# Retention attention and two feed-forward layers on one core: all attention ahead, and a second product that follows its first by two slices

## The chip, the cores and the metric

The kernel runs on one core of one Trainium2 chip. The metric is device microseconds of one execution, the median of several runs. The engines are named as the profile names them: PE does matrix products (PEld is its weight loads), DVE and POOL do elementwise work, ACT does activations and copies, SP issues the transfers (DMA).

## What is computed

A retention attention (2 batches, 8 heads, 768 positions, head size 64) is followed by two feed-forward layers over the 1536 resulting tokens of 512 features, with 2048 hidden features each. Cut to what matters:

```python
state = gamma * state + outer(k[:, :, t], v[:, :, t])     # for each t, batch and head
y[:, :, t] = scale * (q[:, :, t] @ state)
x = y as (1536 tokens, 512)
h = x @ w_in;   g = h * sigmoid(h);         x = g @ w_out      # layer 0
h = x @ w_in;   g = maximum(0.01 * h, h);   out = g @ w_out    # layer 1
```

## The kernel before, in words

**Attention** goes in 12 chunks of 128 positions, six of batch 0 and then six of batch 1. For a chunk, `scores` makes k times q on PE (16 small products), `masked` multiplies them by the decay mask `M` on DVE into `P`, `values` makes P times v, then state times q (not in the first chunk of a batch), then the state's increment k times v (not in the last chunk). `prep` scales q by `G` and k by `KD` on POOL, and a third POOL instruction (line 216) decays the state. `state` and `store_x` are the endings on DVE and ACT: the new state, and the output split into a rounded part `xh` and a rest `xl`. The chunk's q, k and v come in two halves of 512 KB into a ring of four chunks (`att_t`).

**The feed-forward part** treats the tokens as three sets of 512 and the hidden features as 16 slices of 128. For a layer, set and slice, `up` is the first product (12 matmuls of 512 columns, since both operands are split into a rounded part and a rest and three of the four combinations are taken), `act` is the activation on ACT and the split of its result `g` (rest on DVE), `down` is the second product (12 matmuls, four groups of three). After slice 15, `finish` takes the four sums away.

**Weights** arrive as 64-bit numbers, one block of 512 KB for a slice and product. `load_w` fetches a block into one of three stages `ws`, `words` takes its two words on ACT, `conv` makes a 32-bit number of them in four DVE instructions (lines 140, 144, 148, 152), `split_w` splits it (copy on ACT, line 157, and rest on DVE, line 158). `keep_w` writes the split block to scratch in DRAM, and later sets of the same layer read it back with `fetch_w`. There are 64 blocks to convert.

**The order** is written out by hand: each engine runs what the program lists for it, one after the other. Four chunks of attention come first. Then steps `s` follow: step `s` has the first product number `s` (layer, set, slice counted through), and the second product number `s - 20` (`LAG` is 20). The remaining eight chunks are woven into steps 0 to 16, one for two steps. The first 16 steps thus use 16 new blocks, one for each `up`, and there is no second product before step 20. The slots for `g` (20) and for weights (9) are two rings of equal tiles; eight of these tiles are the attention's ring before.

Of the kernel before, what the change touches and what calls it, by code (L numbers as in the profile page):

```python
# [18 lines left out]
C = 128  # L19
# [10 lines left out]
NU = 2 * SETS * NF  # L30
NA = 2 * (NCHUNK - CS)
LAG = NF + 4
WARM = 16
# [9 lines left out]
def retention_moe_kernel(ctx: ExitStack, tc: tile.TileContext, att, w1, w2, cst, out):  # L43
# [21 lines left out]
    cs = const.tile([128, NCST], F32, name="cs")  # L65
# [5 lines left out]
    G = cs[:, o + H + NP:NCST]  # L71
    M = const.tile([128, 2, NP * C], F32, name="M")

    st = [const.tile([128, NP, D], F32, name=f"st{i}") for i in range(2)]
# [6 lines left out]
    gring = [gs.tile([128, 2, T], FR, name=f"g{i}") for i in range(NF)]  # L81
    wring = [gs.tile([128, 2, 512], FR, name=f"w{i}") for i in range(5)]

    def widen():
        a = [gs.tile([128, 2, 512], FR, tag=f"r{i}", name=f"gw{i}") for i in range(8)]
        gring.extend(a[:4])
        wring[0:0] = a[4:]

    def next_w():
        wring.append(wring.pop(0))  # L90
        return wring[-1]
# [9 lines left out]
    def att_t(n, i):  # L101

        return raw[n % 4 * 2 + i // 2][:, i % 2]

    def load_att(n, *halves):
        for i in halves:
            nc.sync.dma_start(out=raw[n % 4 * 2 + i], in_=att[n, :, 2 * i:2 * i + 2])
# [13 lines left out]
    def fetch_w(w):  # L121
        W[w] = next_w()
        nc.sync.dma_start(out=W[w].bitcast(F32), in_=scr[w])
# [30 lines left out]
    def split_w(w):  # L154
        r = rs.pop(w)[0].bitcast(F32)
        t = W[w] = next_w()
        nc.scalar.activation(out=t[:, 0], in_=r, func=AF.Copy)  # L157
        nc.vector.tensor_tensor(out=t[:, 1], in0=r, in1=t[:, 0].bitcast(F32), op=ALU.subtract)  # L158
# [3 lines left out]
    LATE = 3  # L162

    def prep(n):

        if n >= LATE:
            nc.gpsimd.tensor_tensor(out=att_t(n, 0), in0=att_t(n, 0), in1=G, op=ALU.mult)
        if n % NC != NC - 1:
            k3 = att_t(n, 3).rearrange("p (h d) -> p h d", h=H)
# [4 lines left out]
    def scores(n):  # L174
        q, kT = att_t(n, 0), att_t(n, 1)
        sc = pt[n] = pair(n % 2)
# [6 lines left out]
    def masked(n):  # L183
        P = pp.tile([128, 2, NP * C], F32, tag="P", name="P")
        nc.vector.tensor_tensor(out=P, in0=pt[n], in1=M, op=ALU.mult)  # L185
        pt[n] = P

    def values(n, i):
        q, v = att_t(n, 0), att_t(n, 2)
        first = n % NC == 0  # L190
        P = pt.pop(n)
        yu[n] = y, u = bank(i), bank(i + 1)
        for p in range(NP):
            c = slice(p * C, p * C + C)
            for r in range(2):
# [3 lines left out]
                    start=(p == 0), stop=(first and p == NP - 1),  # L199
                )  # L200
        if not first:
            for p in range(NP):
                c = slice(p * C, p * C + C)
                for r in range(2):
                    s = slice(64 * r, 64 * r + 64)
                    nc.tensor.matmul(  # L206
                        out=y[s, c], lhsT=st[0][s, p, :], rhs=q[s, c],
                        start=False, stop=(p == NP - 1),
                    )
        if n % NC == NC - 1:  # L210
            return

        kn = att_t(n, 3)
        u = u[:, 0:NP * D].rearrange("p (a d) -> p a d", a=NP)
        if not first:
            nc.gpsimd.tensor_tensor(
                out=st[1], in0=st[0], in1=GC.unsqueeze(2).to_broadcast([128, NP, D]), op=ALU.mult
            )
        for p in range(NP):
            for r in range(2):  # L220
                c = slice((2 * p + r) * D, (2 * p + r) * D + D)
                nc.tensor.matmul(
                    out=u[64 * r:64 * r + 64, p, :], lhsT=kn[:, c], rhs=v[:, c], start=True, stop=True
                )

    def state(n):
        if n % NC == NC - 1:
            return
        u = yu[n][1][:, 0:NP * D].rearrange("p (a d) -> p a d", a=NP)
        if n % NC:  # L230
            nc.vector.tensor_tensor(out=st[0], in0=st[1], in1=u, op=ALU.add)
        else:
            nc.vector.tensor_copy(out=st[0], in_=u)

    def store_x(n):
        b, c = divmod(n, CS)
        y = yu.pop(n)[0].rearrange("p (a i) -> p a i", a=NP)
        h, l = (x[b][:, :, c * C:c * C + C] for x in (xh, xl))
        if n < LATE:
# [10 lines left out]
    hs, ys = {}, []  # L250

    def place(u):

        return u // (SETS * NF), u // NF % SETS, u % NF

    def up(u):
        layer, b, f = place(u)
        w = W.pop((layer, 0, f))
        h = hs[u] = bank(2 + u % 2)
# [9 lines left out]
    def act(u):  # L269
        g = gring[u % LAG]  # L270
        h = hs.pop(u)
        gf = gp.tile([128, T], F32, tag="gf", name="gf")
        for t in (gf, g[:, 0, :]):
            if place(u)[0] == 0:
# [7 lines left out]
    def down(u, m):  # L282

        layer, b, f = place(u)
        w, g = W[layer, 1, f], gring[u % LAG]
        if u == 0:
# [10 lines left out]
    def finish(u, m):  # L297
        layer, b, f = place(u)
# [7 lines left out]
        r0 = b * T + m * 128  # L306
# [3 lines left out]
        nc.sync.dma_start(out=out[r0:r0 + 128, :], in_=o)  # L310
# [3 lines left out]
    uses = {}  # L314
    for u in range(NU):
        layer, b, f = place(u)
        uses.setdefault(u, []).append((b == 0, (layer, 0, f)))
        uses.setdefault(u + LAG, []).append((b == 0, (layer, 1, f)))
    NS = NU + LAG

    def split_at(s):
        return [w for new, w in uses.get(s, []) if new]

    def weights(s):

        for w in split_at(s + 4):
            load_w(w)
        for w in split_at(s + 1):
            keep_w(w)
# [144 lines left out]
```

## Time and profile before

| what | before |
|---|---|
| median of 3 runs | 598.32 us (598.28 to 598.65) |
| the profiled execution | 598.46 us |
| its span in the trace | 596.3 us |
| PE busy | 576.2 us, 97% of the span |
| DVE busy | 296.8 us, 50% |
| ACT busy | 230.2 us, 39% |
| POOL busy | 31.0 us, 5% |

The profiled execution is 0.14 us above the median, and 2.16 us of it lie outside the span. Shares are averages over stages that differ: DVE's 50% is made of a stretch in which it hardly rests and a long one in which it mostly waits. PE's busy time counts a matmul up to its modelled end, and ends overlap the next ones, so the time of one matmul is read from where the next begins.

### The profile page before, as it was taken

What the parts mean: (1) busy time and instruction counts of PE and PEld (TensorE: products, weight loads), DVE (VectorE), ACT (ScalarE), POOL (GpSimd) and SP (SyncE); (2) the same over time, 40 slices, a digit from 0 to 9 for tenths busy, and PEclk for the clock granted to TensorE, in tenths of its full rate; (3) what the DMA queues carried; (4) which work ended last, traced back from release to release, by engine and by line L of the source; (5) the groups of instructions that cost most, each with busy time, mean ns of one, the idle gap of its engine ahead of it and who ended that gap; (6) DMA issues with size and microseconds to landing.
All of it is one profiled execution on the core that took longest, in us unless ns stands there. A gap on an engine that the chain in (4) does not pass through costs nothing.

```text
span 596.3 us, 8059 instructions
## 1 busy us (share of the span) xinstructions
PE 576.2 (97%) x3024; PEld 474.0 (79%) x3024; DVE 296.8 (50%) x486; ACT 230.2 (39%) x422; POOL 31.0 (5%) x31
## 2 busy tenths in 40 slices
PE   8669898999999999999999999999999999999997
PEld 6558777888888888888888888888888788888885
DVE  3789999496666320136586632586665211011001
ACT  1247564465545321144555422654553222111001
POOL 2450242000000000000000000000000000000000
PEclk9889999999999999999999999999999999999999
DMA  8879983889886765657699777398876685551921
GB/s 322 336 248 321 338 294 143 317 309 359 287 284 219 250 246 198 222 201 274 220 328 325 245 266 282 132 363 309 290 282 213 234 293 189 199 177 59 392 79 71
DMA packets 42231, 150.82 MB, mean 253 GB/s; under 512 B 4688, under 2 KB 4688, under 8 KB 42192
## 3 DMA queue, kind: packets, MB, share of 16 engines
q1 hardware_dynamic: 42048, 149.97, 71.1%
q8 instruction: 24, 0.39, 0.3%
q10 hardware_dynamic: 144, 0.34, 0.2%
q14 instruction: 15, 0.12, 0.1%
HBM read 113.58 MB, written 36.70 MB: 252 GB/s over the span
## 4 chain that ended last, share of the span: by engine, by line
PE 83%; DVE 9%; DMA 5%; issue 1%; ACT 1%; POOL 0%; DVEq 0%; SPq 0%; ACTq 0%
PE b L263 37%; PE p L292 22%; PE b L292 22%; DVE w L158 2%; DMA att_t<-att_dram 2%; DVE r L148 2%; DVE P L185 1%; DMA scr<-w 1%; DVE r L144 1%; DVE r L152 1%; PE b L197 1%; DMA cs<-cst_dram 1%; PE b L206 1%; DMA out_dram<-ob 1%; DVE xl L246 1%
## 5 line engine op out<-in xcount | busy, mean ns | idle before, releaser
L263 PE MATMUL b<-xh,w 128*128 128x512 f32 x488 | 161.1, 394 | 5.0 <-ACT w L157 2.7
L278 DVE TENSOR_TENSOR g<-gf,g 128x512 fp32r<-128x512 f32 x80 | 55.5, 693 | 136.8 <-ACT g L277 91.6
L263 PEld LDWEIGHTS b<-xh,w 128*128 128x128 f32 x488 | 92.1, 189 | 26.0 <-ACT w L157 3.1
L263 PE MATMUL b<-xl,w 128*128 128x512 f32 x244 | 95.7, 392 | 0.0
L263 PE MATMUL b<-xh,gw 128*128 128x512 f32 x280 | 91.9, 389 | 0.0
L277 ACT ACTIVATE gf<-b 128x512 f32<-128x512 f32 x48 | 28.7, 598 | 133.4 <-PE b L263 133.4
L275 ACT ACTIVATE gf<-b 128x512 f32<-128x512 f32 x48 | 28.5, 594 | 94.7 <-PE b L263 92.5
L263 PEld LDWEIGHTS b<-xh,gw 128*128 128x128 f32 x280 | 52.5, 188 | 10.9
L263 PE MATMUL b<-xl,gw 128*128 128x512 f32 x140 | 54.5, 389 | 0.0
L263 PEld LDWEIGHTS b<-xl,w 128*128 128x128 f32 x244 | 46.2, 189 | 9.4
L148 DVE SCALAR_TENSOR_TENSOR r<-ws,r 128x512 int32<-128x512 int32 x64 | 45.8, 715 | 2.2
L152 DVE CUSTOM_DVE_ANT_0 r<-r,u 128x1024 uint16<-128x1024 uint16 x64 | 45.3, 707 | 2.7
L133 ACT ACTIVATE r<-ws 128x512 f32<-128x512 f32 x64 | 43.1, 673 | 4.5 <-DVE w L158 4.2
L158 DVE TENSOR_TENSOR w<-r,w 128x512 fp32r<-128x512 f32 x43 | 34.1, 793 | 20.4 <-ACT w L157 19.2
L134 ACT ACTIVATE u<-ws 128x512 int32<-128x512 uint32 x64 | 42.9, 670 | 0.0
L157 ACT ACTIVATE w<-r 128x512 fp32r<-128x512 f32 x43 | 27.2, 633 | 31.5 <-DVE r L152 31.5
L292 PE MATMUL p<-w,g 128*128 128x512 f32 x144 | 36.9, 390 | 0.0
L292 PE MATMUL b<-w,g 128*128 128x512 f32 x144 | 36.7, 389 | 0.0
L292 PE MATMUL b<-g,w 128*128 128x512 f32 x138 | 35.0, 389 | 0.0
L292 PE MATMUL p<-g,w 128*128 128x512 f32 x138 | 35.0, 389 | 0.0
L292 PEld LDWEIGHTS p<-w,g 128*128 128x128 f32 x144 | 26.9, 188 | 5.9 <-DVE ob L309 0.3
L292 PEld LDWEIGHTS b<-w,g 128*128 128x128 f32 x144 | 27.0, 188 | 5.7
(69 smaller groups left out, 680.6 us busy)
## 6 DMA issues: line engine op xcount, KB each, us to landing
w<-scr SPq DMA_DIRECT2D x71, 512.0 KB, 4.4
ws<-w_dram SPq DMA_DIRECT2D x64, 512.0 KB, 5.1
gw<-scr SPq DMA_DIRECT2D x57, 512.0 KB, 4.3
scr<-w SPq DMA_DIRECT2D x43, 512.0 KB, 3.3
att_t<-att_dram SPq DMA_DIRECT2D x24, 512.0 KB, 7.4
scr<-gw SPq DMA_DIRECT2D x21, 512.0 KB, 3.0
out_dram<-ob SPq DMA_DIRECT2D x12, 256.0 KB, 2.1
cs<-cst_dram ACTq DMA_DIRECT2D x1, 330.0 KB, 5.0
```

What stands on the lines that cost most here:

```text
L133: nc.scalar.activation(out=r.bitcast(F32), in_=t[:, :, 1].bitcast(F32), func=AF.Abs)
L134: nc.scalar.activation(out=u, in_=t[:, :, 0].bitcast(U32), func=AF.Copy, scale=2.0 ** -29)
L144: nc.vector.tensor_scalar(out=r, in0=r, scalar1=3, scalar2=0x3FFFFFF8, op0=ALU.logical_shift_left, op1=ALU.bitwise_and,)
L148: nc.vector.scalar_tensor_tensor(out=r, in0=t[:, :, 1], scalar=-0x40000000, in1=r, op0=ALU.bitwise_and, op1=ALU.bitwise_or)
L152: nc.vector.tensor_tensor(out=r, in0=r, in1=u, op=ALU.add)
L157: nc.scalar.activation(out=t[:, 0], in_=r, func=AF.Copy)
L158: nc.vector.tensor_tensor(out=t[:, 1], in0=r, in1=t[:, 0].bitcast(F32), op=ALU.subtract)
L263: nc.tensor.matmul(out=h, lhsT=w[:, tw, k * 128:k * 128 + 128], rhs=(xh, xl)[tx][b][:, k, :], start=(n == 0), stop=(n == 3 * NP - 1),)
L275: nc.scalar.activation(out=t, in_=h, func=AF.Silu)
L277: nc.scalar.activation(out=t, in_=h, func=AF.Prelu, alpha=0.01)
L278: return lambda: nc.vector.tensor_tensor(out=g[:, 1, :], in0=gf, in1=g[:, 0, :].bitcast(F32), op=ALU.subtract)
L292: nc.tensor.matmul(out=ys[m], lhsT=l, rhs=r, start=(f == 0 and n == 0), stop=(f == NF - 1 and n == 2),)
```

## The change

Attention comes first as a whole, with the batches in turn: chunk 0 of batch 0, chunk 0 of batch 1, chunk 1 of batch 0, and so on (`ORDER`). The sets of the feed-forward part are made of chunks in this new order, and `finish` writes each to its rows. Each batch has its own state. The state's decay becomes a step of its own (`decay`) ahead of `values`. `masked` of the next chunk comes ahead of the conversion and of the chunk's endings. Three weight blocks are converted within attention (in chunks 3, 5 and 7), and three more are loaded there. `G` is no longer part of the constants' transfer on ACT's queue but a transfer of 256 KB on SP's, after the first three halves.

The feed-forward part is a list of 192 products. In the first 16 slices of layer 0, `up` runs for set 0 and for set 1 with the same weight block, one after the other, and `down` of set 0 follows two slices behind; after that one `down` and one `up` alternate, and 18 `down` stand at the end. The blocks read back are 112 where they were 128. Conversion runs five products ahead of use, and so does the reading back. Slots for `g` and for weights come from one list of 29 free tiles, taken in the order in which they became free. Core of the diff:

```diff
-NU = 2 * SETS * NF
-NA = 2 * (NCHUNK - CS)
-LAG = NF + 4
-WARM = 16
+ORDER = [b * NC + c for c in range(NC) for b in range(B)]
+WARM = 20
+LATE = 3
+LAG = 2
+SPLIT = 5
+FETCH = 5
...
-    gring = [gs.tile([128, 2, T], FR, name=f"g{i}") for i in range(NF)]
-    wring = [gs.tile([128, 2, 512], FR, name=f"w{i}") for i in range(5)]
+    free = [gs.tile([128, 2, 512], FR, name=f"s{i}") for i in range(21)]
...
+    ups = [[(l, 0, b, f) for f in range(NF)] for l in range(2) for b in range(SETS)]
+    downs = [(l, 1, b, f) for l in range(2) for b in range(SETS) for f in range(NF)]
+    ahead = [list(t) for t in zip(ups[0], ups[1])]
+    ahead += [[t] for u in ups[2:] for t in u]
+    ops = []
+    for i in range(len(downs) + LAG):
+        ops += downs[i - LAG:i - LAG + 1] if i >= LAG else []
+        ops += ahead[i] if i < len(ahead) else []
...
+        nc.sync.dma_start(out=G, in_=cst[:, ncs:])
...
+        for j in range(NJ):
+            w = early[(j - 3) // 2] if j in (3, 5, 7) else None
+            if j + 1 < NJ:
+                prep(j + 1)
+                scores(j + 1)
+            decay(j)
+            values(j)
+            if j + 4 < NJ:
+                load_att(j + 4, 0, 1)
+            if j in (4, 6, 8):
+                keep_w(early[(j - 4) // 2])
+                load_w(early[(j - 4) // 2 + 3])
+            if w:
+                words(w)
+            if j + 1 < NJ:
+                masked(j + 1)
+            if w:
+                conv(w)
+            store_x(j)
+            state(j)
+            if w:
+                split_w(w)
```

**PE, from the fourth chunk on.** The names: `p` scores, `b` a result bank, `st` the state, `P` the masked scores, `xh` and `xl` the two parts of a set, `w` or `s` a weight tile. Before, the fourth chunk and then the first product:

```order
L181 MATMUL p_321<-att_t 128x128 x8
L197 MATMUL b_330<-P,att_t 64x128 x8
L206 MATMUL b_330<-att_t,st_83 64x128 x8
L222 MATMUL b_331<-att_t 64x64 x8
L263 MATMUL b_384<-xh_85,w_115 128x512
L263 MATMUL b_384<-xl_88,w_115 128x512
```

Now, on PE, the last two chunks and the first product:

```order
L190 MATMUL p_659<-att_t 128x128 x8
L206 MATMUL b_668<-P,att_t 64x128 x8
L215 MATMUL b_668<-att_t,st_84 64x128 x8
L206 MATMUL b_690<-P,att_t 64x128 x8
L215 MATMUL b_690<-att_t,st_86 64x128 x8
L263 MATMUL b_722<-xh_88,s_102 128x512
L263 MATMUL b_722<-xl_91,s_102 128x512
```

Twelve chunks stand ahead of the first product where four stood.

**DVE, around the first conversion of a weight block.** `r` is the number being made, `ws` its stage, `u` its low word. Before, the conversion stands ahead of the state and of the next chunk's mask:

```order
L246 TENSOR_TENSOR xl_88<-yg,xh_85 128x4x128
L140 TENSOR_SCALAR r<-r 128x512
L144 TENSOR_SCALAR r<-r 128x512
L148 SCALAR_TENSOR_TENSOR r<-ws,r 128x512
L152 ISA r<-r,u 128x1024
L231 TENSOR_TENSOR st_83<-st_84,b_225 128x256
L185 TENSOR_TENSOR P<-p_215,M 128x1024
```

Now, on DVE from the mask ahead of the first conversion on:

```order
L194 TENSOR_TENSOR P<-p_308,M 128x1024
L137 TENSOR_SCALAR r<-r 128x512
L141 TENSOR_SCALAR r<-r 128x512
L145 SCALAR_TENSOR_TENSOR r<-ws,r 128x512
L149 ISA r<-r,u 128x1024
L250 TENSOR_TENSOR xl_91<-b_318,xh_88 128x4x128
L237 TENSOR_TENSOR st_86<-st_87,b_319 128x256
L155 TENSOR_TENSOR s_102<-r,s_102 128x512
```

The mask moved ahead of the conversion; the state and the split stand behind it.

**DVE, once the first products run.** `g` and `gf` belong to `act`. Before, in steps with a chunk of attention, from one mask to the next:

```order
L185 TENSOR_TENSOR P<-p_466,M 128x1024
L140 TENSOR_SCALAR r<-r 128x512
L144 TENSOR_SCALAR r<-r 128x512
L148 SCALAR_TENSOR_TENSOR r<-ws,r 128x512
L152 ISA r<-r,u 128x1024
L278 TENSOR_TENSOR g_101<-gf,g_101 128x512
L158 TENSOR_TENSOR w_115<-r,w_115 128x512
L140 TENSOR_SCALAR r<-r 128x512
L144 TENSOR_SCALAR r<-r 128x512
L148 SCALAR_TENSOR_TENSOR r<-ws,r 128x512
L152 ISA r<-r,u 128x1024
L246 TENSOR_TENSOR xl_89<-b_530,xh_86 128x4x128
```

Now, on DVE in the first slices, the instructions of one slice (two `up`, one `down`):

```order
L137 TENSOR_SCALAR r<-r 128x512
L141 TENSOR_SCALAR r<-r 128x512
L145 SCALAR_TENSOR_TENSOR r<-ws,r 128x512
L149 ISA r<-r,u 128x1024
L155 TENSOR_TENSOR s_112<-r,s_112 128x512
L137 TENSOR_SCALAR r<-r 128x512
L141 TENSOR_SCALAR r<-r 128x512
L145 SCALAR_TENSOR_TENSOR r<-ws,r 128x512
L149 ISA r<-r,u 128x1024
L278 TENSOR_TENSOR s_113<-gf,s_113 128x512
L155 TENSOR_TENSOR s_114<-r,s_114 128x512
L278 TENSOR_TENSOR s_115<-gf,s_115 128x512
```

Two conversions and two rests of `g` remain, and the attention's instructions are gone from between them; three products of PE stand beside them where there were two and a chunk.

## Rows read from the trace of the kernel before

**Rows 1.** The page, its first part: busy time, share, instructions of each engine.
```profile
PE 576.2 (97%) x3024; PEld 474.0 (79%) x3024; DVE 296.8 (50%) x486; ACT 230.2 (39%) x422; POOL 31.0 (5%) x31
```

**Rows 2.** Stretches (us from the start): busy of each engine, granted clock, DMA share, GB/s.
```profile
5.00:9.60 4.60, 3.95 (x34) 3.61 (x34) 2.88 (x9) 0.00 (x0) 0.66 (x1) 1.00 1.00 361
9.60:17.70 8.10, 6.82 (x114) 5.91 (x112) 5.45 (x7) 1.79 (x3) 5.46 (x6) 1.00 1.02 403
...
20.70:24.40 3.70, 3.70 (x38) 3.20 (x40) 2.31 (x3) 1.15 (x2) 1.85 (x2) 0.57 1.03 412
...
42.00:112.61 70.61, 66.55 (x617) 53.81 (x616) 64.19 (x100) 41.41 (x75) 13.59 (x11) 1.00 0.79 277
60.00:70.00 10.00, 8.56 (x74) 6.82 (x72) 9.70 (x15) 5.82 (x12) 3.75 (x3) 1.00 0.97 342
112.61:592.40 479.79, 479.54 (x2114) 396.16 (x2112) 204.86 (x345) 177.33 (x328) 0.00 (x0) 1.00 0.70 246
592.40:596.30 3.90, 0.00 (x0) 0.00 (x0) 0.42 (x1) 0.38 (x1) 0.00 (x0) 1.00 0.28 104
```

**Rows 3.** PE in order of time, the opening: start, us, instruction, count [idle before <-releaser].
```profile
5.65 3.98 PE L181 MATMUL p<-att_t 64*128 64x128 f32 x32 [1.00 <-DMA att_t<-att_dram]
9.56 1.41 PE L197 MATMUL b<-P,att_t 128*64 128x128 f32 x16
...
20.68 1.98 PE L197 MATMUL b<-P,att_t 128*64 128x128 f32 x16 [2.92 <-issue]
...
26.68 1.09 PE L197 MATMUL b<-P,att_t 128*64 128x128 f32 x16 [0.68 <-issue]
```

**Rows 4.** PE in order of time, one chunk without waits.
```profile
41.96 1.09 PE L197 MATMUL b<-P,att_t 128*64 128x128 f32 x16
42.99 1.09 PE L206 MATMUL b<-att_t,st 64*64 64x128 f32 x16
44.01 0.69 PE L222 MATMUL b<-att_t 128*64 128x64 f32 x16
44.62 1.16 PE L181 MATMUL p<-att_t 64*128 64x128 f32 x16
45.72 0.50 PE L263 MATMUL b<-xh,w 128*128 128x512 f32 x1
```

**Rows 5.** DVE in order of time, from the mask of one chunk to the next.
```profile
79.30 1.21 DVE L185 TENSOR_TENSOR P<-p,M 128x1024 f32<-128x1024 f32 x1
80.44 0.41 DVE L140 TENSOR_SCALAR r<-r 128x512 f32<-128x512 f32 x1
...
84.07 0.42 DVE L140 TENSOR_SCALAR r<-r 128x512 f32<-128x512 f32 x1
...
87.90 1.78 DVE L158 TENSOR_TENSOR w<-r,w 128x512 fp32r<-128x512 f32 x1
89.60 1.21 DVE L185 TENSOR_TENSOR P<-p,M 128x1024 f32<-128x1024 f32 x1
```

**Rows 6.** All engines in order of time: a conversion on DVE beside POOL's instructions.
```profile
14.94 0.42 DVE L140 TENSOR_SCALAR r<-r 128x512 f32<-128x512 f32 x1
...
15.28 1.27 POOL L167 TENSOR_TENSOR att_t<-att_t,cs 128x512 f32<-128x512 f32 x1 [0.96 <-DMA att_t<-att_dram]
15.39 1.44 DVE L144 TENSOR_SCALAR r<-r 128x512 int32<-128x512 int32 x1
...
18.42 0.69 DVE L152 CUSTOM_DVE_ANT_0 r<-r,u 128x1024 uint16<-128x1024 uint16 x1
...
19.52 0.61 POOL L216 TENSOR_TENSOR st<-st,cs 128x256 f32<-128x256 f32 x1 [1.80 <-DVE st L231]
```

**Rows 7.** POOL in order of time: q and k scaling of one chunk.
```profile
20.23 1.27 POOL L167 TENSOR_TENSOR att_t<-att_t,cs 128x512 f32<-128x512 f32 x1
21.51 1.04 POOL L170 TENSOR_TENSOR att_t<-att_t,cs 128x512 f32<-128x512 f32 x1
```

**Rows 8.** DVE in order of time, later: the split waits for ACT's copy.
```profile
142.90 0.69 DVE L158 TENSOR_TENSOR w<-r,w 128x512 fp32r<-128x512 f32 x1 [0.94 <-ACT w L157]
```

More of the change, by code (lines that the diff above doesn't have):

```diff
@@ L121, in fetch_w @@
     def fetch_w(w):
-        W[w] = next_w()
+        W[w] = free.pop(0)
         nc.sync.dma_start(out=W[w].bitcast(F32), in_=scr[w])
@@ L161, in retention_moe_kernel, with first, last, prep @@
     pt, yu = {}, {}
[L162 to L169, printed above, removed]
+    def first(j):
+        return ORDER[j] % NC == 0
+    def last(j):
+        return ORDER[j] % NC == NC - 1
+    def prep(j):
+        if j >= LATE:
+            nc.gpsimd.tensor_tensor(out=att_t(j, 0), in0=att_t(j, 0), in1=G, op=ALU.mult)
+        if not last(j):
+            k3 = att_t(j, 3).rearrange("p (h d) -> p h d", h=H)
             nc.gpsimd.tensor_tensor(
@@ L172, in prep, with decay, scores @@
             )
-    def scores(n):
-        q, kT = att_t(n, 0), att_t(n, 1)
-        sc = pt[n] = pair(n % 2)
+    def decay(j):
+        if not first(j) and not last(j):
+            s0, s1 = st[ORDER[j] // NC]
+            nc.gpsimd.tensor_tensor(
+                out=s1, in0=s0, in1=GC.unsqueeze(2).to_broadcast([128, NP, D]), op=ALU.mult
+            )
+    def scores(j):
+        q, kT = att_t(j, 0), att_t(j, 1)
+        sc = pt[j] = pair(j % 2)
         for p in range(NP):
@@ L181, in scores, with masked, values @@
                 nc.tensor.matmul(out=sc[:, r, c], lhsT=kT[s, c], rhs=q[s, c], start=True, stop=True)
-    def masked(n):
+    def masked(j):
         P = pp.tile([128, 2, NP * C], F32, tag="P", name="P")
[L185 to L192, printed above, removed]
+        nc.vector.tensor_tensor(out=P, in0=pt[j], in1=M, op=ALU.mult)
+        pt[j] = P
+    def values(j):
+        q, v, kn = (att_t(j, i) for i in (0, 2, 3))
+        s0 = st[ORDER[j] // NC][0]
+        P = pt.pop(j)
+        yu[j] = y, u = [bank(j % 2 * 2 + i) for i in range(2)]
         for p in range(NP):
@@ L198, in values @@
                     out=y[64 * r:64 * r + 64, c], lhsT=v[:, h * D:h * D + D], rhs=P[:, r, c],
-                    start=(p == 0), stop=(first and p == NP - 1),
+                    start=(p == 0), stop=(first(j) and p == NP - 1),
                 )
-        if not first:
+        if not first(j):
             for p in range(NP):
@@ L342, in retention_moe_kernel @@
         nc.scalar.activation(out=z[:, 0:1], in_=z[:, 0:1], func=AF.Silu)
+        early = [weight[i] for i in range(len(ops)) if new[i]][:7]
         load_att(0, 0)
@@ new lines, in retention_moe_kernel @@
+        words(early[3])
+        widen()
+        for i, op in enumerate(ops):
+            l, p, b, f = op
+            if i >= len(ops) - LAST:
+                break
+            for w in at(i + SPLIT + 4, is_new):
+                if w not in early[:6]:
+                    load_w(w)
+            for w in at(i + SPLIT - 1, is_new):
+                if w not in early[:3]:
+                    keep_w(w)
+            for w in at(i + FETCH, is_old):
+                fetch_w(w)
+            if p == 0:
+                up(l, b, f)
+            else:
+                for m in range(4):
+                    down(m, l, b, f)
+                    if f == NF - 1:
+                        finish(m, l, b, f)
+                free.append(gt.pop((l, b, f)))
+            if not kept[i]:
+                free.append(W.pop(weight[i]))
+            for w in at(i + SPLIT, is_new):
+                conv(w)
+            done = i and ops[i - 1][1] == 0
+            if done:
+                rest = act(*ops[i - 1][:1], *ops[i - 1][2:])
+            for w in at(i + SPLIT + 1, is_new):
```

207 lines of the change are left out of this document (70 added, 137 removed).

## The prediction

> **What bounds the kernel now.** I read the page's shares first: PE is busy for 576.2 of 596.3 us [rows 1], so only what PE waits for can be gained. The stretches [rows 2] then part the span in two. From 112.61 us to 592.40 PE runs without a pause that matters: 479.79 us for the 2112 large matmuls listed there (96 `up` and 96 `down` of 12 make 2304; 192 of them lie before 112.61), which is 0.2272 us each. That is PE's own pace, and the change leaves these matmuls as they are. Behind 592.40 lies an ending of 3.90 us. All that can move lies ahead of 112.61.
>
> There PE does 192 large matmuls, worth 192 x 0.2272 = 43.6 us, and all of attention. What attention is worth is read from one chunk that ran without waits [rows 4], from start to start: P times v 1.03 us, state times q 1.02, increment 0.61, scores 1.10. Twelve chunks have the first and the last of these, ten have the two others: 12 x 2.13 + 10 x 1.63 = 41.9 us. So 43.6 + 41.9 = 85.5 us of work took 112.6 us, and 27 us are lost. Take the 43.6 us away, and attention with all losses has cost **69.0 us** so far. This is the number to beat.
>
> Where the loss comes from: in the opening the chunks come at 9.56 and 26.68 us for the first and the fourth `values` [rows 3], (26.68 - 9.56) / 3 = 5.71 us a chunk against some 3.76 us of PE work. After that DVE is the bound: busy for 9.70 of 10 us in the stretch from 60 to 70 [rows 2], and the masks of two neighbouring chunks start at 79.30 and 89.60 [rows 5], 10.3 us apart, while PE has 24 matmuls (5.45 us) and a chunk (3.76) to do, 9.2 us. Two conversions for two first products, and a chunk's endings, are more than DVE can do in PE's time.
>
> **Part 1: the feed-forward part after the change.** In the first 16 slices PE does three products for each slice, 36 x 0.2272 = 8.18 us, and DVE two conversions with two splits and two rests of `g`. A conversion with the rest and the split that follow takes from 80.44 to 84.07, 3.63 us [rows 5]; two are 7.26. One split of the two now has nothing between its conversion and itself, and waits for ACT's copy, for 0.94 us where a row shows that [rows 8]. That makes 8.2 us, about PE's pace, and POOL is idle then. The lead of five products (13.6 us) covers small excesses. I cost this stretch at **nothing**, and its failure is a rival. The 16 blocks fewer to read back hang on nothing that waits: transfers are covered from 112.61 on with 246 GB/s [rows 2]. Slots come free four to five products ahead of their next use, by PE's own progress, also at nothing. Where before 20 steps had a first product alone and 20 a second one alone, now 18 second products stand alone at the end, at the same pace. So the feed-forward part is 2304 x 0.2272 = 523.4 us, and the ending 3.9.
>
> **Part 2: attention in one piece.** Its end T is what has to be built up.
> - PE starts scores at 5.65 us [rows 3], bound by the first transfer and by warming products; both stay. With 41.9 us of work this gives 47.5.
> - The first 32 score matmuls took 3.91 us, up to 9.56 [rows 3], where 2.20 is the full pace [rows 4]: 1.7 us. Four more warming products may take some of it away; I keep **1.7**, with 0 as the other end.
> - Transfers. Before chunk 4 can start, SP's queue holds four chunks (4.19 MB), constants and `G` (0.34), three weight blocks (1.57) and half of chunk 4 (0.52): 6.6 MB. By the stretches some 2.6 MB are in by 9.6 us, and then 403 to 412 GB/s flow [rows 2]: 4.0 / 0.405 = 10 us, landing at 19.6. POOL's scaling of q takes 1.27 [rows 7], so scores of chunk 4 start at 20.9. PE would get there at 18.2: 9.56 + two first `values` of 1.64 + two scores of 1.10, 0.6 of waiting for q of chunk 3 (landing 13.2, scaled at 14.5), and one `values` of 2.66. So the waits are 0.6 + 2.7 = **3.3 us**. From here on a load has two chunks' time (7.5 us) to land.
> - Clock. A wait of 2.92 us before 20.68 was followed by a granted clock of 0.57 for 3.7 us, so mostly the lower of the two levels (1.2 of 2.4 GHz), and P times v took 1.98 us where it took 1.09 [rows 2, 3]. The wait above is nearly as long. The same would cost 1.6 us; between 0 and 1.6 I take **0.8**.
> - DVE beside POOL. A conversion alone takes 2.25 us, and beside POOL the second of its four instructions took 1.44 us instead of 0.43, ending just after POOL's [rows 5, 6]; the conversion lasted from 14.94 to 19.1. POOL has 1.27 + 1.04 + 0.61 = 2.92 us a chunk [rows 6, 7]. If such instructions exclude each other, two chunks with one conversion and split (2.9 us) hold what they share for 2 x 2.92 + 2.9 = 8.8 us, against 7.5 of PE. Three conversions give 3 x 1.3 = **3.8 us**. Lower end 0 (DVE rests for some microseconds ahead of chunk 3, and masks now go ahead of conversions); upper end 3 x 3.0 = 9 us, if each conversion is stretched by 1.8 and each split by 1.1 as in row 87.90 [rows 5, 6], with nothing absorbed.
>
> The Trainium skill, "SBUF — State Buffer", section "Who interferes with whom", says that DVE instructions with two inputs in SBUF, or in a two-port mode, and POOL instructions lock each other out for a whole instruction; the 1.44 us agrees, and what the rule would make of the time if it struck every instruction is rival 4.
>
> Sum: T = 47.5 + 1.7 + 3.3 + 0.8 + 3.8 = **57.1 us**. The first product behind it needs set 0, long stored, a block converted in chunk 3, and a result bank that chunk 11 does not use. So no gap follows.
>
> Time: 57.1 + 523.4 + 3.9 = 584.4 us of span, and 2.16 outside as in the profiled execution (598.46 for 596.3), 586.6 us; that execution was 0.14 above the median, so **586.5 us**. The gain is 69.0 - 57.1 = 11.9 us: DVE's conversions move beside a PE that has three products for each slice instead of two and a chunk.
>
> **Rivals.**
> 1. *DVE falls behind in the first slices.* If both splits wait 0.94 [rows 8], a slice takes 9.14 us of DVE; 16 x 0.96 = 15 us of lag, of which the lead takes 10. Loss some 5 us: 592. For it: 8.2 against 8.18 leaves no room. Against: once DVE is late, ACT's results lie ready, and its waits shrink, as in the gapless rows from 80.44 to 87.90 [rows 5]. Chance 0.08.
> 2. *Transfers bound attention.* Up to the last chunk 16.6 MB pass, with two kept and two more loaded blocks. At 342 GB/s [rows 2] the remaining 14 MB after 9.6 us take 41 us, and with 6.5 us of last work T is 57, no change to the sum. At the 277 of the stretch to 112.61 [rows 2] it is 60.2 + 6.5 = 66.7: 596. Against: that stretch was not at its limit (share 0.79). Chance 0.05, of which half within 0.2% of before.
> 3. *Attention keeps the opening's pace* (slower). At 5.71 us a chunk [rows 3] the last `values` starts at 9.56 + 11 x 5.71 = 72.4 and T is 74.4: 603.8 us. It decides from 5.2 us a chunk on (T of 69.0). For it: the same instructions on the same engines, now with POOL beside all of them. Against: the opening lost most where a conversion stood between scores and mask, and masks go first now; only 3 of 12 chunks have a conversion. Chance 0.02.
> 4. *DVE and POOL exclude each other in full* (slower). If each of a conversion's five instructions waits for a POOL instruction of 1.27 us [rows 7], a block costs 6.3 us and three 19; T is 47.5 + 1.7 + 3.3 + 0.8 + 19 = 72.3, the time 601.6 us. It decides from 5.2 us a block on. Against: from 14.94 to 19.1 the stretch was 1.8 us, two instructions of four [rows 6], since POOL rests a fifth of the time. Chance 0.02.
> 5. *Attention runs at the lower clock* (slower). At the pace of row 20.68 (1.98 for 1.09 us) all 41.9 us become 76, T about 90: 619 us. For it: the fall to 0.57 behind one wait. Against: from 9.60 to 17.70 PE was busy for 6.8 of 8.1 us, with short waits, and the clock stayed at 1.00 [rows 2]. Chance 0.02. The Trainium skill, "TensorE: Matmul & The Clock Gate", section "HAM oscillation — how this bites in real kernels", describes bursts that each start slow again because a transfer is waited for between them; this case is its outcome if every chunk waits.
>
> **How the numbers follow.** The forecast's mechanism has 0.81, with T from 51 (no exclusion, no clock loss, half of the slow start) to 62 (its upper end): 580.5 to 591.5. Rival 1 (0.08) is taken in, and the range ends at 593. Left out are rivals 2 to 5 (0.11) and the tails of the forecast. A difference under 0.2% (1.2 us) is about what a measurement of this kernel cannot tell from none. Faster: 0.81 + 0.08 + half of rival 2 = 0.91; the same 0.03; slower 0.06.
>
> **What would show it.** Right: the first large matmul starts at 51 to 62 us, large matmuls follow each other at 0.227 us from there with pauses of at most 1 or 2 us in all, and the longest wait of PE in attention stands before scores of chunk 4 and behind conversions. Wrong: large matmuls of the first 16 slices waiting for a split or for ACT; scores waiting for a landing in chunk 8 or later; a granted clock near 0.5 over several chunks.

## The result, and the profile after

The changed kernel takes **588.16 us** (587.69 to 589.14, four runs), the kernel before 598.49 beside it: ratio 0.9828, 95% interval 0.9811 to 0.9845, so 1.7% faster. The forecast was 586.5 with a range of 580.5 to 593.0, and faster.

The profiled execution took 588.36 us, 586.2 of them in the span, so 2.16 us lie outside as before. The page's first part, as in [rows 1]:

```profile
PE 571.8 (98%) x3028; PEld 473.0 (81%) x3028; DVE 292.7 (50%) x486; ACT 231.5 (39%) x422; POOL 29.9 (5%) x31
```

Shares say little again: DVE and POOL do what they did. The stretches answer to [rows 2] (from:to, length, then busy time and instructions of PE, PEld, DVE, ACT, POOL, granted clock, DMA share, GB/s):

```profile
59.27:582.30 523.03, 522.87 (x2306) 432.26 (x2304) 250.84 (x425) 217.91 (x400) 0.00 (x0) 1.00 0.67 238
582.30:586.20 3.90, 0.00 (x0) 0.00 (x0) 0.42 (x1) 0.26 (x1) 0.00 (x0) 0.83 0.24 90
25.50:29.50 4.00, 4.00 (x50) 3.43 (x48) 3.93 (x4) 0.56 (x1) 4.00 (x5) 0.63 0.12 44
21.00:25.50 4.50, 2.22 (x18) 2.00 (x20) 0.16 (x2) 0.12 (x1) 3.49 (x4) 0.57 1.02 408
```

The first line is the whole feed-forward part, the 2304 large matmuls in one stretch without a pause: 523.03 us, PE busy for 522.87. The second is the ending, 3.90 us as before. So the first large matmul, which the prediction put at 57.1 us and which had to beat 69.0, starts at 59.27, and that is 9.7 of the span's 10.1 us (596.3 - 586.2); the rest, 0.4, lies in the feed-forward part, whose pace is 0.2270 us a matmul for 0.2272.

What attention lost on its way to 59.27 is read from PE in order of time, as [rows 3, 4] (start, us, instruction, count, idle before it and what ended it):

```profile
5.25 2.43 PE L190 MATMUL p<-att_t 64*128 64x128 f32 x32
8.45 1.09 PE L206 MATMUL b<-P,att_t 128*64 128x128 f32 x16 [0.78 <-DVE P L194]
...
15.40 1.16 PE L190 MATMUL p<-att_t 64*128 64x128 f32 x16 [2.08 <-POOL att_t L169]
16.49 1.09 PE L206 MATMUL b<-P,att_t 128*64 128x128 f32 x16
...
23.28 2.08 PE L190 MATMUL p<-att_t 64*128 64x128 f32 x16 [4.06 <-POOL att_t L169]
25.29 1.97 PE L206 MATMUL b<-P,att_t 128*64 128x128 f32 x16
27.19 1.70 PE L215 MATMUL b<-att_t,st 64*64 64x128 f32 x16
28.82 0.69 PE L224 MATMUL b<-att_t 128*64 128x64 f32 x16
29.44 1.16 PE L190 MATMUL p<-att_t 64*128 64x128 f32 x16
...
50.57 1.09 PE L206 MATMUL b<-P,att_t 128*64 128x128 f32 x16 [0.52 <-DVE P L194]
...
54.09 1.16 PE L190 MATMUL p<-att_t 64*128 64x128 f32 x16 [0.78 <-POOL att_t L169]
...
59.27 0.50 PE L263 MATMUL b<-xh,s 128*128 128x512 f32 x1
```

Scores of chunk 3 (15.40) and of chunk 4 (23.28) wait for their q. Behind the second wait the scores take 2.01 us to the next start, P times v 1.90 and state times q 1.63, where 1.10, 1.03 and 1.02 are the full pace: 2.4 us more, at a granted clock of 0.57 and then 0.63. From 29.44 on the chunks run at 1.00, with small waits. POOL in order of time shows that the wait at 23.28 was for a landing: POOL itself waited for the transfer of q until 21.96.

```profile
21.96 1.26 POOL L169 TENSOR_TENSOR att_t<-att_t,G 128x512 f32<-128x512 f32 x1 [3.57 <-DMA att_t<-att_dram]
...
43.26 1.47 POOL L169 TENSOR_TENSOR att_t<-att_t,G 128x512 f32<-128x512 f32 x1 [1.71 <-DMA att_t<-att_dram]
```

And DVE in order of time, in one slice of the first 16 (compare [rows 5, 8]):

```profile
85.21 0.69 DVE L155 TENSOR_TENSOR s<-r,s 128x512 fp32r<-128x512 f32 x1 [0.70 <-ACT s L154]
...
88.86 0.69 DVE L155 TENSOR_TENSOR s<-r,s 128x512 fp32r<-128x512 f32 x1
89.83 0.69 DVE L278 TENSOR_TENSOR s<-gf,s 128x512 fp32r<-128x512 f32 x1 [0.28 <-ACT s L275]
...
93.57 0.69 DVE L155 TENSOR_TENSOR s<-r,s 128x512 fp32r<-128x512 f32 x1 [0.70 <-ACT s L154]
```

From 85.21 to 93.57 a slice takes DVE 8.36 us; PE's three products take 8.17. DVE is behind by 0.2 us a slice, some 3 us over 16 slices, and PE does not notice.

### The profile page after: what moved, and what is told of

Its sections match the earlier page's. It is cut to its first block, busy times and chain, and to the rows that moved or that the text cites. A ratio compares the mean times of both kernels' runs of the same rounds, so it can differ in the third digit from the quotient of the medians.

```text
span 586.2 us, 8042 instructions
## 1 busy us (share of the span) xinstructions
PE 571.8 (98%) x3028; PEld 473.0 (81%) x3028; DVE 292.7 (50%) x486; ACT 231.5 (39%) x422; POOL 29.9 (5%) x31
## 4 chain that ended last, share of the span: by engine, by line
PE 94%; DMA 5%; SPq 0%; POOLq 0%; POOL 0%; issue 0%; DVE 0%; ACT 0%
PE b L263 45%; PE p L291 22%; PE b L291 22%; DMA att_t<-att_dram 5%; PE b L206 1%; PE b L215 1%; PE p L190 1%; PE b L224 0%; POOLq L472 0%; POOL att_t L169 0%; SPq L104 0%; SPq L351 0%; DVE ob L307 0%; ACT ob L306 0%; POOLq L169 0%
## 5 line engine op out<-in xcount | busy, mean ns | idle before, releaser
L263 PE MATMUL b<-xh,s 128*128 128x512 f32 x560 | 181.7, 389 | 0.0
L263 PEld LDWEIGHTS b<-xh,s 128*128 128x128 f32 x560 | 105.1, 188 | 22.3 <-issue 0.2
L278 DVE TENSOR_TENSOR s<-gf,s 128x512 fp32r<-128x512 f32 x73 | 50.5, 691 | 135.0 <-ACT s L277 87.7
L263 PE MATMUL b<-xl,s 128*128 128x512 f32 x280 | 109.0, 389 | 0.0
L291 PE MATMUL p<-s,s 128*128 128x512 f32 x288 | 73.2, 389 | 0.0
L291 PE MATMUL b<-s,s 128*128 128x512 f32 x288 | 73.1, 389 | 0.0
L263 PE MATMUL b<-xh,sr 128*128 128x512 f32 x208 | 67.8, 389 | 0.0
L291 PEld LDWEIGHTS p<-s,s 128*128 128x128 f32 x288 | 54.0, 188 | 11.5 <-DVE ob L307 0.3
L291 PEld LDWEIGHTS b<-s,s 128*128 128x128 f32 x288 | 54.1, 188 | 11.2
L263 PEld LDWEIGHTS b<-xl,s 128*128 128x128 f32 x280 | 52.6, 188 | 10.8
```

The lines of the kernel that those rows point to most:

```text
L263: nc.tensor.matmul(out=h, lhsT=w[:, tw, k * 128:k * 128 + 128], rhs=(xh, xl)[tx][b][:, k, :], start=(n == 0), stop=(n == 3 * NP - 1),)
L278: return lambda: nc.vector.tensor_tensor(out=g[:, 1, :], in0=gf, in1=g[:, 0, :].bitcast(F32), op=ALU.subtract)
L291: nc.tensor.matmul(out=ys[m], lhsT=l, rhs=r, start=(f == 0 and n == 0), stop=(f == NF - 1 and n == 2),)
```

## The experiments

Each is the changed kernel with one edit, or with several where it says so, timed beside the kernel before. "Attention" below is the start of the first large matmul in the profiled execution.

| kernel | median us | ratio to before (95%) | attention us |
|---|---|---|---|
| the changed kernel | 588.16 | 0.9828 (0.9811 to 0.9845) | 59.27 |
| e1, products in the old order | 599.4 | 1.0009 (0.9994 to 1.0023) | 59.49 |
| e2, unpaired, two slices behind | 645.74 | 1.0784 (1.0761 to 1.0808) | 61.48 |
| e3, one batch after the other | 588.95 | 0.9832 (0.9817 to 0.9846) | 59.92 |
| e4, weights loaded later | 585.01 | 0.9781 (0.9746 to 0.9816) | 60.00 |
| e5, PE kept busy in the wait | 587.11 | 0.9804 (0.9787 to 0.9822) | 57.92 |
| e7, one more DVE instruction | 600.27 | 1.0024 (1.0012 to 1.0037) | 58.09 |
| e8, e4 and q of two chunks off POOL | 585.63 | 0.9783 (0.9763 to 0.9804) | 56.23 |
| e9, k not scaled | 587.24 | 0.9797 (0.9775 to 0.9818) | 58.42 |
| e10, later transfers moved back | 587.64 | 0.9806 (0.9792 to 0.9821) | 59.34 |
| e11, e8 and e10 together | 585.0 | 0.9765 (0.9751 to 0.9778) | 57.08 |
| e12, e11 with k not scaled | 583.03 | 0.9732 (0.9718 to 0.9745) | 54.63 |

The last column is one execution each, and it has a spread of its own. In e1, e2 and e7 the instructions of attention are those of the changed kernel (e1 converts other blocks there, of the same size), and yet it ends at 59.49, 61.48 and 58.09 us. From the scores of chunk 5 to the first large matmul the changed kernel takes 29.83 us, and these three take 30.71, 32.36 and 30.20. On that stretch PE waits for P alone in e1 and e2 (2.8 and 3.0 us), for q alone in e7 (2.3), and for both in the changed kernel (0.5 and 1.3). So a difference of 1 or 2 us in this column, or one kind of wait in place of the other, is no effect of an edit by itself.

### Which part of the change is the gain?

**e1**: attention first, but the feed-forward part in its old order.

```diff
-LAG = 2
-SPLIT = 5
+LAG = NF + 4
+SPLIT = 3
-    ahead = [list(t) for t in zip(ups[0], ups[1])]
-    ahead += [[t] for u in ups[2:] for t in u]
+    ahead = [[t] for u in ups for t in u]
-            for w in at(i + SPLIT + 4, is_new):
+            for w in at(i + SPLIT + 3, is_new):
```

> Attention first as in the changed kernel, but the feed-forward part in the old order: one set after the other, a second product 20 slices behind its first. Theory (the pairing is what lets the conversions hide): attention still ends at about 59.3 us; then one new weight block is needed for each 2.73 us of PE while DVE needs 3.64 us for one (80.44 to 84.07 in the trace of before), so products 4 to 15 wait, 6 to 10 us in all: 594 to 598 us. Rival (it is enough that attention is out of DVE's way): 588 us, as the changed kernel.

599.4 us, no gain at all. Attention ends as early as in the changed kernel, and all of it is given back behind it. PE in order of time, e1, from the fourth first product on:

```profile
68.61 0.50 PE L263 MATMUL b<-xh,s 128*128 128x512 f32 x1 [0.62 <-ACT s L275]
72.25 0.50 PE L263 MATMUL b<-xh,s 128*128 128x512 f32 x1 [0.61 <-ACT s L275]
...
108.79 0.50 PE L263 MATMUL b<-xh,sr 128*128 128x512 f32 x1 [0.63 <-ACT s L275]
```

Twelve `up`s start 3.65 us apart, DVE's time for one conversion, rest and split ([rows 5]: 3.63), where PE needs 2.72: 12 x 0.92 = 11 us, the loss (537.8 us behind the first large matmul, 526.9 in the changed kernel). What PE waits for is ACT taking the sum out of its result bank (line 275), not the weight block. ACT in order of time, e1:

```profile
70.60 0.63 ACT L154 ACTIVATE s<-r 128x512 fp32r<-128x512 f32 x1 [0.92 <-DVE r L149]
71.13 0.58 ACT L275 ACTIVATE gf<-b 128x512 f32<-128x512 f32 x1
71.61 0.59 ACT L275 ACTIVATE s<-b 128x512 fp32r<-128x512 f32 x1
```

ACT's list holds the copy of a later block (line 154) ahead of the activation, that copy waits 0.92 us for DVE, and the two banks of the first product fill; PE starts at 72.25, when the second read of the sum is done. So PE feels DVE's lag after three products already, long before the blocks made in advance are used up.

**e2**: only the pairing undone, the second product still two slices behind. `SPLIT`, `ahead` and the line with `SPLIT + 3` as in e1, and only the last product is finished apart.

```diff
-LAST = 3
+LAST = 1
```

> The changed kernel without the pairing alone: second products two slices behind, but one set after the other, so a slice has two products (5.45 us of PE) and two new blocks. Theory (DVE needs 7.3 to 8 us for a slice): 16 slices lose 1.8 to 2.6 us each, 29 to 41 us, less a lead of some 8: 610 to 622 us, with PE waiting for splits in the first 16 slices. Rival (conversions have room beside PE): 588 to 592 us.

645.74 us, some 24 us beyond the upper end of what was expected. Nor does PE wait for splits, as was expected: 40.9 us of its waits, 27 of them, are for the rest of `g` on DVE (line 278), ahead of `down`. Stretches of e2, and under them the second one in the changed kernel:

```profile
110.00:160.00 50.00, 39.86 (x168) 30.68 (x166) 43.01 (x76) 32.01 (x55) 0.00 (x0) 1.00 0.96 295
330.00:460.00 130.00, 108.47 (x462) 85.28 (x461) 105.38 (x184) 79.11 (x139) 0.00 (x0) 1.00 0.83 260
```
```profile
330.00:460.00 130.00, 130.00 (x575) 107.70 (x574) 73.59 (x125) 61.19 (x111) 0.00 (x0) 1.00 0.77 271
```

In the first, PE is busy for 39.86 of 50 us. The second was missed in the expectation: unpaired, the new blocks of `up` and `down` coincide again in layer 1, whose first set has 16 slices with two conversions for two products. PE needs 5.45 us for such a slice, DVE 7.33, as the splits of one and the next show (DVE in order of time, e2; in the slices of layer 0):

```profile
102.40 0.69 DVE L155 TENSOR_TENSOR s<-r,s 128x512 fp32r<-128x512 f32 x1
...
109.73 0.69 DVE L155 TENSOR_TENSOR sr<-r,sr 128x512 fp32r<-128x512 f32 x1 [0.15 <-ACT sr L154]
```

The pairing therefore helps twice: three products for two conversions in layer 0, and new blocks spread out in layer 1. From e1 and e2, attention first alone is worth nothing, and the order of the products is what turns it into time. Both also shorten the lead of the conversions from five products to three. That this makes the loss is not likely, since DVE's time for a block in e1, and for a slice in e2, is above PE's, but no run has the old order with a lead of five. Nor was the new order run with attention woven in as before.

**e3**: one batch after the other.

```diff
-ORDER = [b * NC + c for c in range(NC) for b in range(B)]
+ORDER = list(range(NCHUNK))
```

> The changed kernel with attention's chunks in the old order, batch 0 and then batch 1. Theory (the turn of the batches hides the state's chain): each chunk's state is needed by the very next chunk, and where a conversion stands ahead of it on DVE (chunks 3, 5, 7) PE waits 2 to 3 us for it; attention ends 4 to 8 us later: 592 to 596 us. Rival (PE waits for loads and POOL in any case, and the chain fits beside scores and P times v): 588 us.

588.95 us, a ratio of 0.9832 against 0.9828: the rival held. With neighbouring chunks of one batch PE did wait for the state, 2.0 us in two waits, the longer one here (PE in order of time, e3):

```profile
47.88 1.09 PE L215 MATMUL b<-att_t,st 64*64 64x128 f32 x16 [1.76 <-DVE st L237]
```

but the waits for q before scores came to 5.9 us where they were 7.5. The turn of the batches is worth nothing that these runs can tell.

**e7**: DVE's rest of `g` taken twice in the first 16 slices, 32 instructions of 0.69 us more, for the question how much room DVE has there.

```diff
+        def rest():
+            for _ in range(2 if layer == 0 and b < 2 else 1):
+                nc.vector.tensor_tensor(...)
```

> The changed kernel with the rest of g taken twice (same result) in the first 16 slices: 1.38 us more of DVE for each slice. Theory (there is no room: 8.0 us of DVE for a slice of 8.18 us): the lag grows by 1.2 us a slice, 19 us, less a lead of 10: 595 to 599 us. Rival (waits of DVE shrink as it falls behind, so that it needs 7.3 us + 1.4 = 8.7): 8 us of lag are covered by the lead: 588 to 590 us.

600.27 us, 12.1 us over the changed kernel. PE in order of time, e7:

```profile
91.71 0.50 PE L263 MATMUL b<-xh,s 128*128 128x512 f32 x1 [0.59 <-ACT s L275]
...
100.97 0.50 PE L263 MATMUL b<-xh,s 128*128 128x512 f32 x1 [0.62 <-ACT sr L275]
```

A slice now takes 9.3 us, 1.1 above PE's 8.17; 16 x 1.1 = 17.6 us of lag cost 12.1, so the lead swallows about 5.5 us, and not the 10 that rival 1 reckoned. The waits are again for ACT's emptying of a result bank, as in e1.

### What did attention lose, and to what?

The theory by now: the load of chunk 4 lands late since three weight blocks stand ahead of it, and PE's clock falls behind that wait. The rival: POOL and DVE lock each other out, and loads moved earlier give nothing.

**e4**: the first three weight blocks are loaded behind chunks 4, 5 and 6.

```diff
-        for w in early[:3]:
-            load_w(w)
...
+            if j < 3:
+                load_w(early[j])
```

> The changed kernel with the first three weight blocks loaded behind chunks 4, 5 and 6 and not ahead of chunk 4 (1.57 MB less ahead of it on SP's queue). Theory (the wait of 4.1 us before the scores of chunk 4 is for bytes ahead of it in the queue, and the fall of the clock after it, 2.4 us, comes from that wait): chunk 4 lands 3.8 us earlier, no clock loss; 588.2 - 6 = 582 us. Rival (the ring of four chunks and POOL give the wait back at later chunks): 586 to 588 us.

585.01 us (584.39 to 589.0), half of what was expected. The profiled execution was the slowest of the four. POOL in order of time, e4, and then PE:

```profile
18.03 1.27 POOL L169 TENSOR_TENSOR att_t<-att_t,G 128x512 f32<-128x512 f32 x1 [0.65 <-DMA att_t<-att_dram]
```
```profile
15.41 1.60 PE L190 MATMUL p<-att_t 64*128 64x128 f32 x16 [2.10 <-POOL att_t L169]
...
20.73 1.16 PE L190 MATMUL p<-att_t 64*128 64x128 f32 x16
...
31.65 1.09 PE L206 MATMUL b<-P,att_t 128*64 128x128 f32 x16 [2.26 <-DVE P L194]
...
53.24 1.86 PE L190 MATMUL p<-att_t 64*128 64x128 f32 x16 [2.14 <-POOL att_t L169]
```

Q of chunk 4 landed by 18.03 where it was 21.96, so 3.9 us earlier, as expected, and its scores wait for nothing now and start 2.55 us earlier. But a wait for P, behind a conversion on DVE, appears at 31.65, and one for q at 53.24. The granted clock also fell three times, to 0.64, 0.60 and 0.54 over stretches of some 4 us from 15.41, 32.67 and 53.24; by the starts of the instructions this cost about 4.7 us, and this execution lies 4.0 above the median. So in this execution the clock and later limits took back what the load gave; in the median half of what was expected is left.

**e5**: the wait stays, but PE does 32 products of zeros in it (that the zeros `z` get a tile of their own is left out here).

```diff
+FILL = {4: 32}
...
+        for i in range(FILL.get(j, 0)):
+            nc.tensor.matmul(out=sc[:, 0, 0:256], lhsT=z[:, 0:128], rhs=z, start=True, stop=True)
```

> The changed kernel with 32 small bf16 products on zeros put on PE ahead of the scores of chunk 4, into the bank that these scores then overwrite (3.4 us in the wait of 4.1 us). Theory (the fall of the granted clock behind that wait costs 2.4 us by itself): scores to state product of chunk 4 run at full pace, and attention ends 2 to 2.4 us earlier: 586 us. Rival (the slow products only use up a wait that follows anyway, for loads or POOL): 588 us, with the same first large matmul at 59 us.

587.11 us. PE in order of time, e5:

```profile
19.15 3.67 PE L189 MATMUL p<-z 128*128 128x256 bf16 x32
23.12 1.16 PE L194 MATMUL p<-att_t 64*128 64x128 f32 x16 [0.30 <-POOL att_t L171]
26.87 1.16 PE L194 MATMUL p<-att_t 64*128 64x128 f32 x16
...
50.08 1.09 PE L210 MATMUL b<-P,att_t 128*64 128x128 f32 x16 [1.59 <-DVE P L198]
```

The scores of chunk 4 start as late as ever, those of chunk 5 2.57 us earlier than in the changed kernel (26.87 for 29.44), at a granted clock of 1.00: the clock cost 2.4 us. At the end attention is 1.35 us shorter, with waits for P behind conversions of 3.1 us in three. E1 and e2 show such waits without this edit, so they are not shown to be what took back the rest, and the intervals of e5 and of the changed kernel overlap.

**e8**: e4, and q of chunks 3 and 4 no longer scaled on POOL; their outputs are scaled on DVE, as those of the first three chunks.

```diff
-LATE = 3
+LATE = 5
```

> The late weights of the run before, and for chunks 3 and 4 the factor G is applied by DVE on the result and not by POOL on q (as for chunks 0 to 2). Theory (the first waits of attention are load plus POOL's 1.3 us, and DVE rests there): the waits at chunks 3 and 4 shrink to under 1 us, the clock stays up: attention ends at 53 to 55 us, 582 to 584 us. Rival (what is won is given back at later chunks, where DVE's conversions and POOL exclude each other): 585 us, as with late weights alone.

585.63 us; the rival held. Attention ends at 56.23 us in the profiled execution, with 3.5 us of waits for P in three places. Whether this step adds to e4 can't be told from the medians.

**e9**: POOL's scaling of k is left out, so that a part of the computation is missing; 1.04 us of POOL for each of ten chunks.

> The changed kernel without POOL's scaling of k by KD (this part of the computation is left out): POOL has 1.9 us a chunk and not 2.9. Theory (from chunk 5 on the time that is lost, 2.1 us, comes from DVE and POOL excluding each other): conversions are stretched less, P and scores come in time, attention ends 1.5 to 2.5 us earlier, and the waits at chunks 3 and 4 stay: 586 us. Rival (these late waits are for loads): 588 us.

587.24 us, attention 0.85 us shorter, both within the spread. POOL in order of time, e9:

```profile
42.36 1.27 POOL L169 TENSOR_TENSOR att_t<-att_t,G 128x512 f32<-128x512 f32 x1 [3.15 <-DMA att_t<-att_dram]
```

With less to do POOL waits longer for its transfers (3.15 us here), and PE's late waits for q stay. In this execution they are waits for loads, then, not for POOL.

**e10**: the blocks written back and the next three loads, which stand between the attention's loads, are issued behind the last of them.

```diff
-            if j in (4, 6, 8):
-                keep_w(early[(j - 4) // 2])
-                load_w(early[(j - 4) // 2 + 3])
+            if j == 7:
+                load_w(early[3])
+                load_w(early[4])
+            elif j == 8:
+                load_w(early[5])
+                for i in range(3):
+                    keep_w(early[i])
```

> The changed kernel, with the write-back of the first three blocks and the loads of the next three issued on SP only behind the loads of the last chunk (they stood between the loads of chunks 8 and 11). Theory, formed from the run without k scaling (the late waits of attention, 2 us, are for landings of chunks 8 to 11, behind 1 MB of weights each): POOL's scaling of q in chunks 10 and 11 starts earlier, the waits before the last three scores go, attention ends 1 to 2 us earlier: 586.5 to 587 us. Rival (my forecast: DVE and POOL exclude each other): 588 us, with the waits before scores and P unchanged.

587.64 us: about nothing. All late waits for q are gone (4.8 us in two remain, before chunks 3 and 4), and one for P stands in their place (PE in order of time, e10, with chunk 3 first):

```profile
15.37 1.70 PE L190 MATMUL p<-att_t 64*128 64x128 f32 x16 [2.08 <-POOL att_t L169]
...
51.50 1.09 PE L206 MATMUL b<-P,att_t 128*64 128x128 f32 x16 [1.62 <-DVE P L194]
```

From chunk 5 to the first large matmul 29.38 us passed, 29.83 in the changed kernel. In e1 the late waits for q are absent too, with a wait for P of 1.82 us at the same place, and there the transfers were not moved. So this exchange is not shown to be the edit's doing.

**e11** is e8 and e10 together, **e12** is e11 without POOL's scaling of k (the same part of the computation left out as in e9).

> All three moves: weights behind the chunks they stood ahead of, write-backs and next loads at the end, G by DVE in chunks 3 and 4. Theory (loads are the limit everywhere): attention ends at 51 to 53 us, 580 to 582 us. Rival (with loads early, chunks 3 to 8 are bound by DVE's conversions beside POOL, each stretched to 4 us): P waits of 1 to 2 us remain in three chunks, attention ends at 54 to 56 us: 583 to 585 us.

> The kernel with all three moves, without POOL's scaling of k (this part of the computation is left out). If conversions beside POOL are what remains: the waits for P shrink and attention ends 2 to 3 us earlier than with the three moves alone. If loads or PE remain: the same time as with the three moves, within 0.5 us.

e11 takes 585.0 us, 3 us less than the changed kernel and the fastest complete version of these (its interval and those of e4 and e8 overlap). The loads are nearly out of the way (waits of 0.8 and 0.9 us before chunks 3 and 5), and what is left are waits for P, 4.9 us in three, the longest of them here (DVE and POOL in order of time, e11, and then PE):

```profile
21.36 1.26 POOL L169 TENSOR_TENSOR att_t<-att_t,G 128x512 f32<-128x512 f32 x1 [0.47 <-DMA att_t<-att_dram]
21.80 1.10 DVE L137 TENSOR_SCALAR r<-r 128x512 f32<-128x512 f32 x1
22.65 1.15 POOL L172 TENSOR_TENSOR att_t<-att_t,cs 128x512 f32<-128x512 f32 x1
...
22.94 1.15 DVE L141 TENSOR_SCALAR r<-r 128x512 int32<-128x512 int32 x1
23.77 0.79 POOL L179 TENSOR_TENSOR st<-st,cs 128x256 f32<-128x256 f32 x1
24.12 0.98 DVE L145 SCALAR_TENSOR_TENSOR r<-ws,r 128x512 int32<-128x512 int32 x1
25.17 1.27 POOL L169 TENSOR_TENSOR att_t<-att_t,G 128x512 f32<-128x512 f32 x1 [0.61 <-DMA att_t<-att_dram]
25.25 1.74 DVE L149 CUSTOM_DVE_ANT_0 r<-r,u 128x1024 uint16<-128x1024 uint16 x1
```
```profile
31.10 1.09 PE L206 MATMUL b<-P,att_t 128*64 128x128 f32 x16 [3.44 <-DVE P L194]
32.12 1.78 PE L215 MATMUL b<-att_t,st 64*64 64x128 f32 x16
```

The conversion lasts from 21.80 to 26.99, 5.2 us where it takes 2.25 alone, and the next mask stands behind it. Each of its four instructions ends 0.3 to 0.6 us behind the end of a POOL instruction (22.62, 23.80, 24.56, 26.44), as if it had waited for that. e12, with about a third less on POOL, takes 583.03 us; attention is 2.45 us shorter, and the longest wait for P is 1.63 us. The same edit gave 0.9 us in e9, when loads still came late, and that is not clear of the spread; the 2.0 us between e11 and e12 are. The Trainium skill, "SBUF — State Buffer", section "Who interferes with whom", calls this an exclusive lock between DVE and POOL; the rows above agree. The 2.0 us are not the bare price of the exclusion: behind the wait of 3.44 us PE's clock fell in e11 (0.60 from 32.10 to 36.39, about 1.5 us lost), while e12 ran at 1.00, and the edit also takes POOL's waits for k out of its list.

So two limits lie close together in attention: loads, and conversions beside POOL, and a wait for either can bring the clock down. Which of them comes last differs between executions of the same instructions, and taking away the clock loss alone (e5), POOL's work alone (e9) or the late transfers alone (e10) gave no more than the spread. What is clear of it is e8 and e11 against the changed kernel, and e12 against e11. Not tried: conversions moved out of attention altogether.

## Why the prediction was right, and where its terms were off

The mechanism held. Attention alone lies ahead, PE then runs 2304 matmuls without a pause, and DVE's conversions go beside three products for a slice (first large matmul forecast between 51 and 62 us, measured 59.27). That the order of the products is the cause is shown by e1 and e2. The terms:

| term of the sum | predicted | measured |
|---|---|---|
| start of scores, and 41.9 us of work | 47.5 | 47.15 (scores at 5.25) |
| slow first scores | 1.7 | 1.0 |
| loads | 3.3 | 6.4 |
| clock | 0.8 | 2.4 |
| DVE beside POOL | 3.8 | 2.1 lost from chunk 5 on, 1.3 of it in waits for q |
| first large matmul | 57.1 | 59.27 (0.2 in small gaps) |
| feed-forward part | 523.4 | 523.03 |
| ending | 3.9 | 3.90 |
| outside the span | 2.16 | 2.16 |

- **Slow first scores.** With 20 warming products the 32 score matmuls took 2.43 us, 3.91 before [rows 3]; 0.78 us of waiting for the first P came in place of it. No run isolates the warming products.
- **Loads**, the largest miss. The wait before chunk 3 was 2.1 us, forecast 0.6, and the one before chunk 4 4.1 us, forecast 2.7, with 0.2 before chunk 2. The step that failed: q of chunk 4 was put at 19.6 us by adding up what stands ahead of it in SP's list, 6.6 MB. It landed at about 21.9, and some 7.6 MB had moved by then (349 GB/s from 0 to 21.9), so about 1.0 MB issued behind it had moved before it was complete; why, no run isolates. In e4, with the blocks out of the way, chunk 4 waited for nothing. (The time at which PE gets there, 18.2, adds up to 18.3.) The sentence that a load has two chunks' time to land from here on was off as well: DMA idles from 25.5 to 29.5 (share 0.12, 44 GB/s) because the ring's next slot comes free behind the late chunk, and q of chunks 9 to 11 came late once more (0.28, 0.27 and 0.78 us). That was named as a sign of a wrong forecast, and it came to 1.3 us, not all of it the landings': POOL's scaling of q for chunks 9 and 10 took 1.47 and 1.62 us for 1.27, beside DVE, and in e1 and e2 there are no such waits.
- **Clock.** Both ends of the bounds, 0 and 1.6, were below the measured 2.4 us. They came from one row that showed 3.7 us at the low clock; this time the wait was longer (4.06 for 2.92 us) and 5.5 us of work ran mostly at the lower level (1.2 of 2.4 GHz). e5 confirms the size.
- **DVE beside POOL.** 29.83 us passed from 29.44 to 59.27 for 27.76 us of work: 2.1 us lost instead of 3.8, and of these 1.3 were waits for q and 0.5 waits for P. The exclusion is there, for the first conversion lasted from 26.55 to 31.27, 4.7 us for 2.25. But PE was still held up by its long wait and its low clock, and felt little of it. The loss is not a fixed amount either: on the same stretch the same attention lost 2.95 us in e1, 4.6 in e2 (with a fall of the clock) and 2.4 in e7, in e1 and e2 with waits for P alone. So 3.8 lies within what was seen, and that it was too much is shown for the one profiled execution only.
- The errors had both signs, and +3.1, +1.6, -1.7, -0.7 and -0.35 with 0.2 of gaps leave +2.2 on the first large matmul. The forecast of the time is nearer than its parts are, and that is in part luck: loads and clock cost 4.7 us more than forecast, and the other terms happened to give 2.75 back.

**The rivals.** Rival 1 (DVE behind) did not strike: the slice takes DVE 8.36 us, one split of two waits (0.70, forecast 0.94), and its lag of some 3 us in all fits within the lead. But e7 shows how near it was, and that its lead of 10 us was too large: about 5.5 are there, because two result banks and ACT's order limit it, not the blocks made in advance. Rival 2 (transfers) struck in part, early and not as a rate: 238 GB/s suffice from 59 us on. Rivals 3 and 4 did not come: the chunks behind 29.44 passed at 3.75 us at first and at 5.2 only once, near the end (48.89 to 54.09). Rival 4 decides from 5.2 us of added time for a block; the longest conversions of all runs, 5.2 us in all in e4 and e11, are 3 us longer than one alone. Rival 5 struck for one stretch of 5.5 us. The Trainium skill, "TensorE: Matmul & The Clock Gate", section "HAM oscillation — how this bites in real kernels", tells of products that start slow behind a wait for a transfer; the stretch behind 23.28 agrees, and e5 shows that products of no use are a remedy.

## What to carry to other kernels

When one engine prepares operands for another, count both engines' time over one period of the order (here two conversions per slice against two products or three) before moving other work about: attention first gave nothing until the period fitted. A lead in prepared operands is worth only as much as the results that can be parked meanwhile; look for what the consumer actually waits for (here a result bank that a third engine empties late). Where a removed wait gives half of what it cost, look for a second limit just behind it, and take both away in one run before believing either price. And before a microsecond of one trace is explained, look at other executions of the same instructions: here their waits and their clock differed by more than that.

## What was not expected of the hardware

- The granted clock did not fall behind equal waits alike. Before the scores of chunk 3, PE waited 2.08 us in the changed kernel and ran them at the full pace (1.09 us to the next start); in e10, with the same instructions up to there and the same wait of 2.08, they took 1.70. Of eight executions with a wait of 1.97 to 2.26 us at this place, four ran slowly in that chunk (e1, e4, e7, e10) and four did not (the changed kernel, e2, e5, e9). The four runs of e4 spread over 4.6 us.
- A load's landing is not the sum of what was issued ahead of it: chunk 4's half came some 2.3 us after that sum at about 405 GB/s, while 408 GB/s flowed (21.0 to 25.5).
- A chain of four DVE instructions beside a busy POOL was stretched from 2.25 to 5.2 us (e4, e11), in e11 the last of them, 0.69 us alone [rows 6], to 1.74.
